# Two shared SBUF tags padded to 4608 bytes, so that the operands of the wide matmuls begin at one byte of a 512-byte line

## The chip, the cores and the metric

The kernel runs on one core of one Trainium2 chip. The metric is the device time of one execution in microseconds (us); lower is better. A core has a matrix engine (TensorE, PE in the profile, with its weight loads shown apart as PEld), VectorE (DVE), ScalarE (ACT), GpSimd (POOL) and SyncE (SP, which issues most of the DMAs here). SBUF, the on-chip memory that engines read their operands from, has 128 partitions; every tile is a run of bytes at the same start address in each of them.

## The reference, cut to what matters

Three stages follow each other on 8 x 3072 = 24576 rows of 256 values:

```
scores = (z @ z.T) / S;  attn = max(scores, 0)**2;  x = u * (attn @ v)         # S = 3072, z is 64 wide
xn = x / rms(x) * rms_g                                                        # 256 -> 1536 -> 256
x = (silu(xn @ w_gate) * (xn @ w_val)) @ w_out
keep = (x @ w_skip) > 0;  e = argmax(x @ gate);  p = softmax(x @ gate)[e]      # 8 experts, 256 -> 1024 -> 256
out = x;  out[keep] = x[keep] + p * (max(x[keep] @ w1[e], 0) @ w2[e])
```

## The kernel before, in words

The 24576 rows are worked in 48 chunks of 512 rows (CH). Every float32 operand of a large product is split into a rounded high part and the rest as a low part (`split`), and one product is three matmuls on TensorE (`mm3`, lines 231 to 233): high weights on high data, high weights on low data, low weights on high data. In each, the stationary operand (the weights) is a 128x128 tile, 512 bytes in each partition, and the moving operand is 512 columns wide, 2048 bytes in each partition. The score product (lines 566 and 567, `s<-z,z`) is two matmuls of the same shape. TensorE loads the weights of the next matmul while the one before it streams its moving operand.

The order is software-pipelined by hand: `Stream.unit` runs a front part (first product and its evictions) and, two units later, the back part (second product). The chunks go attention 0, attention 1, first MoE 0, attention 2, first MoE 1 and so on to first MoE 47. The profile's names for their matmuls:

- attention: 12 units for a chunk, each 4 matmuls `s<-z,z` and 12 matmuls `acc<-a,v` (moving `a`, weights `v`)
- first MoE: 12 units for a chunk, each 12 matmuls `gv<-xn,wg_s` and `gv<-xn,wv_s` (moving `xn`) and 6 matmuls `yacc<-h,wo_s` (moving `h`)
- second MoE (from about 4660 us on): groups, one per expert, with tiles of 512 and 256 rows, each with `h<-xh,w` (moving `xh`) and `y<-h,w` (moving `h`). Groups with an even number keep their weights in the tag `vhl`, odd ones in the tag `wodd` of the pool `p2`.

Tiles are given a tag in a pool. A tag gets as many buffers as `bufs` says, each as large as the largest tile that ever asks for that tag, and the tags of a pool lie one behind the other. So the size of one tag sets where every later tag begins. Of the pool `sp`, in the order of their places: `acct`, `u`, `vhl` (6 buffers; split `v`, the weights of even groups, `xh`, and `xn` of the last chunk), `zcat`, `stage`, `z1`, `z2` (the operands of the scores), `x`, `xn`, `hl` (5 buffers; `a` and `h`). Behind it lies the pool `wp` (`wg_s`, `wv_s`, `wo_s`), whose room the pool `p2` takes over for the second MoE.

Nearly all tags are whole multiples of 512 bytes. The tags `u` and `x` are 4096 bytes in almost all uses, but the first group of the second MoE loads its rows into them (line 888): 4 rows of XW = 265 values, 4240 bytes, and 4240 = 8 x 512 + 144 (the tags are laid out in steps of 32 bytes, so 4256 = 8 x 512 + 160 bytes lie between the start of `u` and of the next tag). The bytes below address 16384 of each partition are scratch in which GpSimd's own DMAs (`indirect_dma_start`, lines 703 and 945: the scatters into `xs` and `out`) keep their descriptors.

Of the kernel before, what the change touches and what calls it, by code (L numbers as in the profile page):

```python
# [10 lines left out]
F32 = mybir.dt.float32  # L11
# [9 lines left out]
P = 128  # L21
# [49 lines left out]
def tile_relu2_attention_moe_moe2(  # L71
# [15 lines left out]
    nc = tc.nc  # L87
# [15 lines left out]
    XW = D + E + 1  # L103
# [19 lines left out]
    sp = ctx.enter_context(tc.tile_pool(name="sp", bufs=1))  # L123
# [17 lines left out]
    for q, tag in ((0, "acct"), (1, "u")):  # L141
        g0, g1 = 4 * q, min(NCB, 4 * q + 4)
        if g0 < g1:
            t = sp.tile([P, g1 - g0, KT, DQ], F32, tag=tag, name=f"z0_{q}", bufs=1)
# [700 lines left out]
    class Group:  # L845
# [39 lines left out]
        def load_x(self, t):  # L885
            n = self.sizes[t] // P
            if self.i == 0 and t < 2:
                xt = sp.tile([P, n, XW], F32, tag=("u", "x")[t], name=f"xt_{self.i}_{t}", bufs=1)
            else:
                tag, bufs = ("xt", 3) if n == KT else ("xts", 5)  # L890
                xt = pools["p2"].tile([P, n, XW], F32, tag=tag, name=f"xt_{self.i}_{t}", bufs=bufs)
            if isinstance(self.e, int):
                r = self.e * RE + sum(self.sizes[:t])
            else:
                r = self.dyn(0, E * RE - TS)
            nc.sync.dma_start(xt, xs[ds(r, self.sizes[t]), :].rearrange("(p k) w -> p k w", k=n))
            self.xt[t] = xt
# [279 lines left out]
```

## Time and profile before

| | us |
|---|---|
| median of 3 runs | 5281.31 (5280.94 to 5281.61) |
| the profiled execution, its own time | 5281.5 |
| span of its instructions | 5279.6 |
| TensorE busy in the span | 5197.5 (98%), 23724 matmuls and transposes |
| weight loads busy | 4260.4 (81%) |
| VectorE, ScalarE, GpSimd busy | 3578.2 (68%), 2701.8 (51%), 426.8 (8%) |

How to read it: matmuls are pipelined, so the busy time of one matmul (about 390 ns) is longer than the time after which the next one starts (about 227 ns), and they overlap. The pace of a row of matmuls is the difference of their start times in the timeline. The granted clock is the share of TensorE's full clock that the chip granted; over the whole span it was 0.994.

### The profile page before, as it was taken

The page shows a single profiled execution, that of the slowest core. Times are in us where ns is not written, and L with a number is a line of the kernel's source. Part 1 is how long each engine was busy: PE and PEld are TensorE (multiplying, and loading weights), DVE is VectorE, ACT ScalarE, POOL GpSimd, SP SyncE. Part 2 cuts the span into 40 slices and gives each one's busy share as a digit, 9 for nine tenths or more (in the row PEclk, how much of TensorE's full clock was granted, in tenths as well). Part 3 has the DMA queues.
Part 4 walks back from the last instruction along what each step waited for, and adds up shares of the span by engine and source line. Part 5 has one row for each costly group of instructions (what it writes and reads, how often), then busy time and mean ns, then how long its engine had stood idle before and what let it go on. Part 6 is the DMA issues. An engine that isn't in the chain of part 4 may idle for free. (4 is left out here: it accounts for less than half of the span.)

```text
span 5279.6 us, 65890 instructions
## 1 busy us (share of the span) xinstructions
PE 5197.5 (98%) x23724; PEld 4260.4 (81%) x23724; DVE 3578.2 (68%) x8966; ACT 2701.8 (51%) x3559; POOL 426.8 (8%) x428
## 2 busy tenths in 40 slices
PE   7899999999999999999999999999999999999998
PEld 5688888888888888888888888878888888888888
DVE  8666767676677766776667667776677666544455
ACT  6445545465464554555546545455465554433344
POOL 5100000000000000000000000000000000021111
PEclk9999999999999999999999999999999999999999
DMA  5201101020011110111102001111011110122224
GB/s 163 54 19 41 43 20 36 19 62 23 19 36 35 41 27 19 42 43 23 32 19 66 19 19 36 38 40 25 19 42 43 24 31 18 41 85 84 79 95 155
DMA packets 547841, 234.43 MB, mean 44 GB/s; under 512 B 422357, under 2 KB 528000, under 8 KB 547384
## 3 DMA queue, kind: packets, MB, share of 16 engines
q1 hardware_dynamic: 533496, 205.00, 15.8%
q0 software_dynamic: 14016, 25.21, 1.4%
q8 instruction: 186, 3.05, 0.2%
q14 instruction: 143, 1.17, 0.1%
HBM read 144.79 MB, written 99.30 MB: 46 GB/s over the span
## 5 line engine op out<-in xcount | busy, mean ns | idle before, releaser
L738 ACT ACTIVATE gr<-gv 128x512 f32<-128x512 f32 x576 | 343.9, 597 | 1187.4 <-PE gv L233 1187.4
L232 PE MATMUL acc<-a,v 128*128 128x512 f32 x2304 | 916.6, 398 | 12.3 <-DVE a L228 8.5
L233 PE MATMUL acc<-a,v 128*128 128x512 f32 x2304 | 916.4, 398 | 0.0
L231 PE MATMUL acc<-a,v 128*128 128x512 f32 x2304 | 912.5, 396 | 1.6 <-ACT acct L427 1.6
L569 ACT ACTIVATE r<-s 128x1024 f32<-128x1024 f32 x576 | 590.9, 1026 | 339.2 <-PE s L567 319.8
L228 DVE TENSOR_TENSOR a<-r,a 128x512 fp32r<-128x512 f32 x1128 | 737.9, 695 | 23.4 <-ACT a L227 4.0
L654 DVE CUSTOM_DVE_ANT_0 jk<-ytok,wrb 128x256 bf16<-128x256 f32 x1656 | 697.9, 421 | 35.2
L739 DVE TENSOR_TENSOR gr<-gr,gv 128x512 f32<-128x512 f32 x576 | 394.8, 685 | 456.8 <-ACT gr L738 453.3
L228 DVE TENSOR_TENSOR h<-gr,h 128x512 fp32r<-128x512 f32 x576 | 399.1, 693 | 395.6 <-ACT h L227 395.6
L227 ACT CAST h<-gr 128x512 fp32r<-128x512 f32 x576 | 357.5, 621 | 573.8 <-DVE gr L739 573.8
L570 ACT ACTIVATE r<-r 128x1024 f32<-128x1024 f32 x576 | 611.5, 1062 | 18.2
L703 POOL DMA_INDIRECT xs<-ytok,pu x192 | 208.2, 1084 | 4128.3 <-DVE pu L701 3082.6
L232 PEld LDWEIGHTS acc<-a,v 128*128 128x128 f32 x2304 | 435.6, 189 | 120.1 <-DVE a L228 11.5
L231 PEld LDWEIGHTS acc<-a,v 128*128 128x128 f32 x2304 | 434.5, 189 | 107.0 <-ACT acct L427 2.1
L233 PEld LDWEIGHTS acc<-a,v 128*128 128x128 f32 x2304 | 434.6, 189 | 102.5
L225 DVE CAST a<-r 128x512 fp32r<-128x512 f32 x564 | 238.9, 424 | 379.1 <-ACT r L570 378.6
L231 PE MATMUL gv<-xn,wg_s 128*128 128x512 f32 x1152 | 457.0, 397 | 13.4 <-DVE gr L739 13.3
L567 PE MATMUL s<-z,z 128*128 128x512 f32 x1152 | 455.2, 395 | 0.1
L232 PE MATMUL gv<-xn,wg_s 128*128 128x512 f32 x1152 | 450.6, 391 | 1.1 <-DVE xn L228 1.1
L233 PE MATMUL yacc<-h,wo_s 128*128 128x512 f32 x1152 | 450.3, 391 | 0.6 <-POOL wo_s L376 0.6
L233 PE MATMUL gv<-xn,wg_s 128*128 128x512 f32 x1152 | 450.0, 391 | 0.0
L232 PE MATMUL yacc<-h,wo_s 128*128 128x512 f32 x1152 | 449.9, 391 | 0.0
(200 smaller groups left out, 9036.5 us busy)
## 6 DMA issues: line engine op xcount, KB each, us to landing
raw<-in_moe_w_dram SPq DMA_DIRECT2D x76, 512.0 KB
vn<-in_v_dram SPq DMA_DIRECT2D x48, 512.0 KB
out_dram<-ytok SPq DMA_DIRECT2D x48, 512.0 KB
ys<-yb SPq DMA_DIRECT2D x368, 64.0 KB
ytok<-ys SPq DMA_DIRECT2D x46, 512.0 KB
u<-in_u_dram SPq DMA_DIRECT2D x360, 64.0 KB
xs<-pad SPq DMA_DIRECT2D x8, 1325.0 KB
xt<-xs SPq DMA_DIRECT2D x16, 530.0 KB
```

The lines of the kernel that those rows point to most:

```text
L225: nc.vector.tensor_copy(hi, src)
L227: nc.scalar.copy(hi, src)
L228: (nc.vector if lo_eng == "v" else nc.gpsimd).tensor_sub(lo, src, hi.bitcast(F32))
L231: nc.tensor.matmul(ps, w_hi, x_hi, start=start, stop=False)
L232: nc.tensor.matmul(ps, w_hi, x_lo, start=False, stop=False)
L233: nc.tensor.matmul(ps, w_lo, x_hi, start=False, stop=stop)
L567: nc.tensor.matmul(ps[:, t], zj, zi2, start=False, stop=True)
L569: nc.scalar.activation(out=r, in_=ps, func=AF.Relu)
L570: nc.scalar.activation(out=r, in_=r, func=AF.Square)
L654: nc.vector.tensor_tensor_reduce(out=junk, in0=ytok[:, k, :D], in1=wrb[:, e, :], op0=ALU.mult, op1=ALU.add, scale=1.0, scalar=0.0, accum_o ...
L738: nc.scalar.activation(out=r[:, 0], in_=ps[:, 0], func=AF.Silu)
L739: nc.vector.tensor_mul(r[:, 1], r[:, 0], ps[:, 1])
```

## The change

The tile of line 888 is asked for as a run of 1152 values (9 x 128) in each partition, 4608 = 9 x 512 bytes, of which the first 1060 values are used as before. So the tags `u` and `x` grow from 4240 to 4608 bytes. The room comes from the scratch of GpSimd's DMAs, which goes from 16384 to 4096 bytes in each partition; everything behind it moves down by 12288 bytes (24 x 512). No instruction is added, removed or moved on any engine; what changes is where tiles lie. In the built programs the tiles begin, in bytes into their partition and, in brackets, into a line of 512 bytes:

| tag (tiles) | before | after |
|---|---|---|
| `r` (evicted scores, `gr`) | 33056 (288) | 20768 (288) |
| `acct` | 42592 (96) | 30304 (96) |
| `u` | 46688 (96) | 34400 (96) |
| `vhl` (`v`, even `w`, `xh`, last `xn`) | 50944 (256) | 39008 (96) |
| `stage` | 102144 (256) | 90208 (96) |
| `z1`, `z2` | 106240, 118528 (256) | 94304, 106592 (96) |
| `x` | 122624 (256) | 110688 (96) |
| `xn` | 126880 (416) | 115296 (96) |
| `hl` (`a`, `h`) | 135072 (416) | 123488 (96) |
| `wg_s`, odd `w` | 155552, 171936 (416) | 143968, 160352 (96) |
| `wv_s` | 180128 (416) | 168544 (96) |
| `wo_s` | 204704 (416) | 193120 (96) |

Buffers of one tag, the slices of 128 weights and the high and low parts lie whole multiples of 512 bytes apart, so the number in brackets holds for all of them. By it, the 128x512 matmuls of before are: `acc<-a,v` moving 416, weights 256; `gv` and `yacc` 416 and 416; `s` 256 and 256; in the second MoE, even groups `h` 256 and 256, `y` moving 416, weights 256; odd groups `h` moving 256, weights 416, `y` 416 and 416; the `gv` of the last chunk moving 256, weights 416. After the change all are 96 and 96.

```diff
@@ -885,7 +885,9 @@
         def load_x(self, t):
             n = self.sizes[t] // P
             if self.i == 0 and t < 2:
-                xt = sp.tile([P, n, XW], F32, tag=("u", "x")[t], name=f"xt_{self.i}_{t}", bufs=1)
+
+                room = sp.tile([P, -(-n * XW // P) * P], F32, tag=("u", "x")[t], name=f"xt_{self.i}_{t}", bufs=1)
+                xt = room[:, : n * XW].rearrange("p (n w) -> p n w", w=XW)
             else:
                 tag, bufs = ("xt", 3) if n == KT else ("xts", 5)
                 xt = pools["p2"].tile([P, n, XW], F32, tag=tag, name=f"xt_{self.i}_{t}", bufs=bufs)
@@ -1158,7 +1160,7 @@
-    nc = _bacc.Bacc("TRN2", target_bir_lowering=False, num_devices=1)
+    nc = _bacc.Bacc("TRN2", target_bir_lowering=False, num_devices=1, dynamic_dma_scratch_size=4096)
```

## Rows read from the trace of the kernel before

**Rows 1.** The page: span; TensorE's busy tenths and granted clock in 40 slices

```profile
span 5279.6 us, 65890 instructions
...
PE   7899999999999999999999999999999999999998
...
PEclk9999999999999999999999999999999999999999
```

**Rows 2.** Waits of TensorE: who, for whom, total us, times, longest

```profile
PE gv L231 <- DVE gr L739: 13.3, 1, 13.3
```

**Rows 3.** TensorE by shape: line, names, shape, count | busy us, mean ns

```profile
L232 PE MATMUL acc<-a,v 128*128 128x512 f32 x2304 | 916.6, 398 | 12.3 <-DVE a L228 8.5 <-POOL a L228 3.8
...
L231 PE MATMUL acc<-a,v 128*128 128x512 f32 x2304 | 912.5, 396 | 1.6 <-ACT acct L427 1.6
L231 PE MATMUL gv<-xn,wg_s 128*128 128x512 f32 x1152 | 457.0, 397 | 13.4 <-DVE gr L739 13.3
L567 PE MATMUL s<-z,z 128*128 128x512 f32 x1152 | 455.2, 395 | 0.1
...
L233 PE MATMUL yacc<-h,wo_s 128*128 128x512 f32 x1152 | 450.3, 391 | 0.6 <-POOL wo_s L376 0.6
...
L231 PE MATMUL yacc<-h,wo_s 128*128 128x512 f32 x1152 | 449.4, 390 | 0.3 <-ACT wo_s L375 0.3
...
L232 PE MATMUL gv<-xn,wv_s 128*128 128x512 f32 x1152 | 448.7, 390 | 0.0
L566 PE MATMUL s<-z,z 128*128 128x512 f32 x960 | 386.8, 403 | 5.5 <-ACT r L569 3.1 <-DVE gr L739 0.3
L231 PE MATMUL y<-h,w 128*128 128x512 f32 x256 | 102.3, 400 | 0.0
...
L232 PE MATMUL h<-xh,w 128*128 128x512 f32 x256 | 100.6, 393 | 0.0
...
L232 PE MATMUL h<-xh,w 128*128 128x256 f32 x288 | 81.3, 282 | 0.0
```

**Rows 4.** Timeline of TensorE, attention of chunk 20: start us, us, line, names

```profile
1959.74 0.39 PE L232 MATMUL acc<-a,v 128*128 128x512 f32 x1
...
1962.31 0.39 PE L566 MATMUL s<-z,z 128*128 128x512 f32 x1
...
1963.23 0.40 PE L231 MATMUL acc<-a,v 128*128 128x512 f32 x1
```

**Rows 5.** Timeline of TensorE, first MoE of chunk 46

```profile
4565.82 0.39 PE L233 MATMUL gv<-xn,wg_s 128*128 128x512 f32 x1
...
4569.22 0.39 PE L233 MATMUL yacc<-h,wo_s 128*128 128x512 f32 x1
```

**Rows 6.** Timeline of TensorE, first MoE of chunk 47

```profile
4625.81 0.39 PE L233 MATMUL gv<-xn,wg_s 128*128 128x512 f32 x1
...
4630.24 0.40 PE L231 MATMUL gv<-xn,wv_s 128*128 128x512 f32 x1
```

**Rows 7.** Stretches: length, busy of PE, PEld, DVE, ACT, POOL, clock, DMA, GB/s

```profile
1960.00:1965.00 5.00, 5.00 (x23) 4.05 (x22) 4.03 (x15) 3.95 (x5) 0.00 (x0) 1.00 0.00 0
...
4560.00:4590.00 30.00, 29.95 (x138) 24.59 (x137) 19.46 (x62) 9.80 (x16) 0.00 (x0) 1.00 0.00 1
4624.00:4654.00 30.00, 30.00 (x136) 24.17 (x135) 13.64 (x24) 11.20 (x17) 9.18 (x6) 1.00 0.08 26
```

**Rows 8.** TensorE by shape in 4760 to 4817 us, group 2

```profile
L233 PE MATMUL y<-h,w 128*128 128x512 f32 x32 | 12.7, 396 | 0.0
...
L233 PE MATMUL h<-xh,w 128*128 128x512 f32 x31 | 12.2, 392 | 0.0
```

**Rows 9.** TensorE by shape in 4820 to 4877 us, group 3

```profile
L233 PE MATMUL y<-h,w 128*128 128x512 f32 x32 | 12.5, 391 | 0.0
L233 PE MATMUL h<-xh,w 128*128 128x512 f32 x31 | 12.3, 397 | 0.0
```

**Rows 10.** GpSimd by line: the scatter into the output, and its idle time

```profile
L945 POOL DMA_INDIRECT out_dram<-ot,xt x100 | 101.0, 1010 | 479.6 <-DVE ot L940 270.1 <-DMA out_dram<-ot,xt 91.0 <-DVE h L981 42.3
```

## The prediction

> **What bounds the kernel now.** I read the page first. TensorE is busy in nine tenths or more of every slice but the first two and the last, and its granted clock is full in all 40 [rows 1]: the kernel is as long as its row of matmuls. The waits come next. The longest single wait of TensorE in the whole run is 13.3 us, once [rows 2]; so what remains is the pace at which one matmul follows another, and every nanosecond of pace counts, some 20,000 times.
>
> The view by shape shows that this pace is not one number. All the matmuls of 128x512 do the same amount of work, and still their mean durations range from 390 ns (`gv` on line 232) to 398 ns (`acc`) [rows 3]. Durations overlap, so I check against the timeline that a longer duration is a slower pace. In the attention of chunk 20 the 11 steps from 1959.74 to 1962.31 us are 2.57 us, 233.6 ns each [rows 4]; in the first MoE of chunk 46 the 15 steps from 4565.82 to 4569.22 us are 3.40 us, 226.7 ns each [rows 5]. 6.9 ns more in pace, against 7 to 8 in duration: the excess of a duration over 390 ns can be read as lost time.
>
> **Is the address the reason?** By the table of places, `gv` and `yacc` before have moving operand and weights at the same byte of a 512-byte line (416), `acc` has 416 against 256. That alone proves nothing, since attention differs in much else. Two places in the trace come close to an experiment.
>
> The first MoE of chunk 47 runs the same lines on the same weights as that of chunk 46, but its `xn` lies in `vhl`, at 256 against weights at 416. Its 19 steps from 4625.81 to 4630.24 us take 4.43 us, 233.2 ns each [rows 6], the pace of `acc`. VectorE is less busy there than in chunk 46 (13.64 us of 30 against 19.46), ScalarE about the same (11.20 against 9.80), the clock is full in both [rows 7]. Six of the 19 are `yacc`, at 416 and 416; had these the fast pace, the other 13 would take 236 ns each, more than any `acc` average, so an equal pair between unequal ones seems not to recover at once. GpSimd (9.18 us) and DMAs (share 0.08) are active there and not in chunk 46; but the attention units at 1960 to 1965 us have neither (0.00 and 0.00) and are slow [rows 7].
>
> In the second MoE the roles change from group to group. In group 2 (even) `h` has 256 and 256 and takes 392 ns, `y` has 416 against 256 and takes 396 [rows 8]. In group 3 (odd) `h` has 256 against 416 and takes 397, `y` has 416 and 416 and takes 391 [rows 9]. The swap follows the addresses and not the stage, and an equal pair is fast at 256 as it is at 416. After the change every pair is 96 and 96.
>
> **The change part by part.** No instruction is added, removed or moved, so no wait is added either. The terms are excesses over 390 ns.
>
> - `acc`: three rows, 912.5 to 916.6 us, together 2745.5 us for 6912 matmuls; 6912 x 0.390 = 2695.7; excess 49.8 us [rows 3]. All of it lies on the path, except in the first two slices, where TensorE is only 7 and 8 tenths busy and waits for other things [rows 1]; two of the 48 attention chunks run there, 2 us. Term: 48 us.
> - `gv`: six rows from 457.0 to 448.7 us, together 2705.1 us, excess 9.4 us; of this the first row (397 ns) alone has 7.7, and its matmuls come first in a unit and also bear the waits [rows 2, 3]. What is due to addresses is the last chunk (144 x 6.5 ns = 0.9 us) and the first matmuls after an `acc` that is still out of step. Between 2 and 9.4 us I take 5.
> - `yacc`: three rows, 449.4 to 450.3 us, 1349.6 in all, excess 1.8 us; I take 2.
> - `s`: equal at 256 before, yet 395 ns on line 567: they stand in fours between slow `acc`, as `yacc` did in chunk 47. Line 567: 455.2 - 1152 x 0.390 = 5.9 us. Line 566 is at 403 ns, 12.4 us over for 960 of its 1152, but it also waits for ScalarE to free the buffer [rows 3]. The timeline has 4 steps of `s` in 0.92 us, 230 ns, so (230 - 226.7) x 2304 = 7.6 us [rows 4]. Between 7.6 and 21 I take 8, the timeline's.
> - wide `h` and `y` of the second MoE: six rows from 102.3 to 100.6 us, 607.7 in all for 1536, excess 8.7 us [rows 3]; the rows of line 231 bear waits too. I take 7.
> - 128x256 matmuls: 1728, at 282 ns in the row shown [rows 3]. No row shows a fast and a slow one side by side. Bounds: nothing, and 7 ns on the half with unequal bytes, 864 x 7 = 6 us. I take nothing.
> - other engines: `r`, `acct` and `u`, from and to which most of the evictions go, keep their byte in the line; `a`, `h`, `v` and `xn` get another one. No row shows VectorE or ScalarE at two bytes for the same operation; I take nothing, and if they lost some time it would be covered: in the busiest attention units VectorE has 4.03 us of 5 and ScalarE 3.95 [rows 7], which at the faster pace become 4.15 and 4.07 of 5. The second product of a unit comes two units behind its first.
> - GpSimd's smaller scratch: scatters could wait for room. In the second MoE GpSimd already waits for the landing of its scatter before it issues the next (91.0 us of idle time), so hardly more than one is under way, and it is idle for 479.6 us between 100 scatters, 4.8 us for each [rows 10]. A wait below that costs nothing but at the very end, behind the last matmul: 0 to some 5 us. I take nothing.
>
> Sum: 48 + 5 + 2 + 8 + 7 = 70 us. The profiled execution took 5281.5 us around its span of 5279.6; 5281.5 - 70 = 5211.5, and as the median of the runs shown is 5281.31, I forecast 5211 us. What is late next is again TensorE, at an even pace of 227 ns.
>
> **The rivals.**
>
> No change. The pace of a stage could be set by what goes on beside TensorE (evictions, DMAs), and the addresses only happen to go with it. Then all terms are nothing: 5281 us. For it: attention does have the most traffic on VectorE and ScalarE. Against it: the pair of chunks 46 and 47, and the swap between groups 2 and 3. The Trainium skill speaks for this rival: TensorE: Matmul & The Clock Gate (Part 2, step by step) says that the weight load and the moving operand have separate read ports, so that loading the next weights takes no bandwidth from the running matmul, and SBUF — State Buffer (Who interferes with whom) says that TensorE never waits on anyone. By these pages no byte address could matter. The trace disagrees: 233.2 against 226.7 ns [rows 5, 6].
>
> Only part of it. Unequal bytes cost what `acc` shows, but `s`, `gv` and the second MoE are slow for other reasons (an evicted buffer, the groups' DMAs): then the gain is that of `acc` alone, 48 us, or less if `acc` settles between the two paces, say at 230 ns: 25 us. 5233 to 5257 us. For it: `s` is slow at 256 and 256.
>
> Slower: byte 96 itself is a bad one. No 512-wide matmul of before reads its operands from byte 96, and what I take for the difference of two bytes could be a property of certain start bytes. If 96 were of the slow kind, `gv`, `yacc` and the half of `h` and `y` now equal would go to the pace of `acc`: (233.3 - 226.7) x (6912 + 3456 + 768) = 73 us more, 5354 us. It decides as soon as an equal pair at 96 is slow. Against it: equal pairs are fast at both bytes where they occur, 256 and 416 [rows 8, 9].
>
> **How the numbers follow.** Forecast (an even pace everywhere) 0.83, part of it 0.08, no change 0.05, byte 96 bad (or the scratch felt beyond all the gain) 0.04. A difference under 0.2% (10.6 us) can't be told from none; so faster 0.91, same 0.05, slower 0.04. The range: with all upper ends (50 + 9.4 + 1.8 + 21 + 8.7 + 6) the gain would be 97 us, 5184; that all come together is unlikely, so 5192. Upward it takes in `acc` alone (5233) and a few us of the scratch: 5238.
>
> **What would show it.** Right: all rows of wide `acc`, `s`, `gv`, `yacc`, `h` and `y` at 389 to 392 ns but for the first of a unit; steps of 227 ns in an attention unit; `yacc` and `gv` as before; chunks 46 and 47 alike; the scatters' idle time on GpSimd shorter by about what TensorE gains and their durations as before. Wrong: `acc` still at 397 ns (traffic, not addresses), or `gv` and `yacc` at 397 (byte 96), or TensorE's pace even but its waits longer by tens of us (the gain given back to VectorE or ScalarE), or waits of GpSimd before each scatter.

## The result, and the profile after

The changed kernel takes 5212.19 us (median of 4 runs, 5209.95 to 5214.61) against 5281.46 us of the kernel before (4 runs, 5280.94 to 5281.82): a ratio of 0.987, 95% interval 0.9858 to 0.9882. The forecast was 5211 us. The execution that was profiled took 5214.61 us around its span, 66.9 us less than the profiled execution of before.

The page first (span; TensorE's busy tenths; its granted clock). It answers to [rows 1]: as many instructions, the same shape of the span, the same clock. Only the length is another.

```profile
span 5212.8 us, 65890 instructions
...
PE   7899999999999999999999999999999999999998
...
PEclk9999999999999999999999999999999999999999
```

TensorE by shape (line, names, shape, count | busy us, mean ns of one | idle before). It answers to [rows 3].

```profile
L232 PE MATMUL acc<-a,v 128*128 128x512 f32 x2304 | 900.3, 391 | 12.7 <-DVE a L228 8.8 <-POOL a L228 3.8
L231 PE MATMUL acc<-a,v 128*128 128x512 f32 x2304 | 899.1, 390 | 1.7 <-ACT acct L427 1.7
L233 PE MATMUL acc<-a,v 128*128 128x512 f32 x2304 | 898.9, 390 | 0.0
L231 PE MATMUL gv<-xn,wg_s 128*128 128x512 f32 x1152 | 455.2, 395 | 13.7 <-DVE gr L739 13.6
L567 PE MATMUL s<-z,z 128*128 128x512 f32 x1152 | 452.4, 393 | 0.1
L233 PE MATMUL yacc<-h,wo_s 128*128 128x512 f32 x1152 | 449.4, 390 | 0.6 <-POOL wo_s L376 0.6
...
L232 PE MATMUL gv<-xn,wv_s 128*128 128x512 f32 x1152 | 448.6, 389 | 0.0
...
L566 PE MATMUL s<-z,z 128*128 128x512 f32 x960 | 385.1, 401 | 5.7 <-ACT r L569 3.1 <-DVE gr L739 0.3
...
L231 PE MATMUL y<-h,w 128*128 128x512 f32 x256 | 101.4, 396 | 0.0
...
L232 PE MATMUL h<-xh,w 128*128 128x512 f32 x256 | 99.8, 390 | 0.0
...
L232 PE MATMUL h<-xh,w 128*128 128x256 f32 x288 | 81.4, 283 | 0.0
```

`acc` fell from between 396 and 398 ns to 390 and 391, the duration that `gv` and `yacc` had before and still have. What stands above that now are the first `gv` and the first `y` of a unit and `s` on line 566, which also wait, and `s` on line 567 at 393 ns. By the starts in the trace, an `s` whose four stands between `acc` takes 226.7 ns from its start to the next one; a four beside `yacc` or beside the small transposes takes 227 to 231.

The timeline of an attention unit (start us, duration us, line, names) answers to [rows 4].

```profile
1929.63 0.39 PE L231 MATMUL acc<-a,v 128*128 128x512 f32 x1
...
1932.35 0.39 PE L566 MATMUL s<-z,z 128*128 128x512 f32 x1
...
1933.26 0.39 PE L231 MATMUL acc<-a,v 128*128 128x512 f32 x1
```

From 1929.63 to 1933.26 us are 16 steps, 12 `acc` and 4 `s`: 3.63 us, 226.9 ns each, where before an `acc` step took 233.6 ns. The first MoE of chunk 47, the slow twin in [rows 6], has become like its neighbour in [rows 5]; from its timeline:

```profile
4565.63 0.39 PE L233 MATMUL gv<-xn,wv_s 128*128 128x512 f32 x1
...
4567.67 0.39 PE L233 MATMUL yacc<-h,wo_s 128*128 128x512 f32 x1
```

9 steps in 2.04 us, 226.7 ns each (before, 233.2).

Little was given back. The longest wait of TensorE, in the view of waits, is 13.6 us [13.3 in rows 2]; in a busy attention unit, in the view of stretches, VectorE and ScalarE have 4.50 and 4.05 us of 5 (the columns are those of [rows 7]), and TensorE is busy for all 5:

```profile
PE gv L231 <- DVE gr L739: 13.6, 1, 13.6
```

```profile
1930.00:1935.00 5.00, 5.00 (x24) 4.14 (x23) 4.50 (x16) 4.05 (x5) 0.00 (x0) 1.00 0.00 0
```

One thing else moved. Behind the last matmul GpSimd ends the program with DRAIN instructions. The view of that line shows count, shortest / median / longest in ns, first and last start; first the kernel before, then after:

```profile
L1173 POOLq DRAIN  x3: 40/103/6601, 5272.2 to 5279.4; - x3
```

```profile
L1175 POOLq DRAIN  x3: 40/103/1619, 5210.3 to 5212.5; - x3
```

The longest fell from 6.60 to 1.62 us, on the path that sets the end. I had not looked at it. The scatters before it (GpSimd by line) wait 85.1 us for their landings where it was 91.0, and take 993 ns where it was 1010 [rows 10]: the small scratch held none of them up.

```profile
L947 POOL DMA_INDIRECT out_dram<-ot,xt x100 | 99.3, 993 | 477.1 <-DVE ot L942 245.6 <-DMA out_dram<-ot,xt 85.1 <-DVE w L228 48.7
```

### The profile page after: what moved, and what is told of

It is laid out like the page before. It is cut to its first block, busy times and chain, and to the rows that moved or that the text cites. A ratio compares the mean times of both kernels' runs of the same rounds, so it can differ in the third digit from the quotient of the medians.

```text
span 5212.8 us, 65890 instructions
## 1 busy us (share of the span) xinstructions
PE 5132.3 (98%) x23724; PEld 4258.5 (82%) x23724; DVE 3576.1 (69%) x8966; ACT 2705.3 (52%) x3559; POOL 427.3 (8%) x428
## 5 line engine op out<-in xcount | busy, mean ns | idle before, releaser
L232 PE MATMUL acc<-a,v 128*128 128x512 f32 x2304 | 900.3, 391 | 12.7 <-DVE a L228 8.8
L231 PE MATMUL acc<-a,v 128*128 128x512 f32 x2304 | 899.1, 390 | 1.7 <-ACT acct L427 1.7
L233 PE MATMUL acc<-a,v 128*128 128x512 f32 x2304 | 898.9, 390 | 0.0
L231 PE MATMUL gv<-xn,wg_s 128*128 128x512 f32 x1152 | 455.2, 395 | 13.7 <-DVE gr L739 13.6
L232 PE MATMUL gv<-xn,wg_s 128*128 128x512 f32 x1152 | 449.4, 390 | 1.1 <-DVE xn L228 1.1
L233 PE MATMUL yacc<-h,wo_s 128*128 128x512 f32 x1152 | 449.4, 390 | 0.6 <-POOL wo_s L376 0.6
L231 PE MATMUL yacc<-h,wo_s 128*128 128x512 f32 x1152 | 449.3, 390 | 0.4 <-ACT wo_s L375 0.4
L232 PE MATMUL yacc<-h,wo_s 128*128 128x512 f32 x1152 | 449.0, 390 | 0.0
```

Of the source, the lines that this page charges most:

```text
L231: nc.tensor.matmul(ps, w_hi, x_hi, start=start, stop=False)
L232: nc.tensor.matmul(ps, w_hi, x_lo, start=False, stop=False)
L233: nc.tensor.matmul(ps, w_lo, x_hi, start=False, stop=stop)
```

## The experiments

The theory: the pace is lost where moving operand and weights lie at different bytes of a line. Rivals: the traffic beside TensorE, byte 96 as such, the scratch, and a shorter line. Where it says "one run" there is a single time; the times of one kernel spread over some 5 us.

### The two halves of the change, and another common byte

Scratch alone: the kernel before with

```diff
+    nc = _bacc.Bacc("TRN2", target_bir_lowering=False, num_devices=1, dynamic_dma_scratch_size=4096)
```

> The smaller scratch alone; the two tags stay at 4240 bytes, so all tiles keep the bytes of before (416, 256, 96). Theory 'equal bytes' (a matmul is fast when moving operand and weights begin at the same byte of a 512-byte line): acc stays at 397 ns, 5281 us, at most 5 us less because GpSimd's drain at the very end (6.6 us before, 1.6 us after) may go with the scratch. Rival 'scratch' (room or reads of the smaller scratch give the gain): 5212 us, acc at 390 ns.

Measured: 5276.26 us (10 runs, 5273.61 to 5278.14) against 5281.79 (19 runs); ratio 0.9989 (0.9979 to 0.9999). By shape, `acc` keeps its slow pace, and in the view of the last line the drain is as short as in the changed kernel:

```profile
L233 PE MATMUL acc<-a,v 128*128 128x512 f32 x2304 | 917.4, 398 | 0.0
```

```profile
L1173 POOLq DRAIN  x3: 40/103/1619, 5272.8 to 5275.0; - x3
```

The scratch by itself brings 5.5 us, of which the drain is 5.0 (6.60 - 1.62).

Padding alone: the changed kernel with a scratch that just leaves it room.

```diff
-    nc = _bacc.Bacc("TRN2", target_bir_lowering=False, num_devices=1, dynamic_dma_scratch_size=4096)
+    nc = _bacc.Bacc("TRN2", target_bir_lowering=False, num_devices=1, dynamic_dma_scratch_size=15360)
```

> The two tags padded, the scratch at 15360 bytes, nearly the default (the whole default does not leave room for the padding); all tiles at byte 96 as in the changed kernel. 'Equal bytes': acc at 390 ns, 5212 us, up to 5 us more if the drain at the end goes with the scratch. 'Scratch': 5281 us.

Measured: 5221.25 us (4 runs, 5217.12 to 5222.15), ratio 0.9883 (0.9867 to 0.9900). The pace is wholly there; what is missing is at the end:

```profile
L233 PE MATMUL acc<-a,v 128*128 128x512 f32 x2304 | 899.9, 391 | 0.0
```

```profile
L1175 POOLq DRAIN  x3: 40/103/7744, 5211.2 to 5219.5; - x3
```

So padding alone brings 60.5 us and the scratch alone 5.5, in sum 66; the whole brought 69.3 (5281.46 - 5212.19). The 3 us between are within the spread, and 1.1 of them lie in the drain, which is longer with 15360 bytes than with 16384 (7.74 against 6.60 us).

All operands at byte 0 instead of 96: the changed kernel with 416 unused bytes ahead of everything.

```diff
-    snap = cpool.tile([P, 2], F32, name="snap")
+    snap = cpool.tile([P, 106], F32, name="snap")[:, :2]
```

> The changed kernel with 416 unused bytes ahead of all tiles of the products, so that every operand begins at byte 0 of a line instead of 96. 'Equal bytes': 5212 us, acc and all wide matmuls at 390 ns as at 96. Rival 'a certain byte' (start bytes are fast or slow by themselves, 96 being a fast one): some rows off 390 ns; if 0 were of the kind of 256 in the scores of before (395 ns), 5215 to 5285 us.

Measured: 5213.95 us (4 runs, 5211.44 to 5214.64), ratio 0.9871 (0.9854 to 0.9887). By shape:

```profile
L233 PE MATMUL acc<-a,v 128*128 128x512 f32 x2304 | 900.0, 391 | 0.0
```

As fast as at 96. Between these two bytes it doesn't matter which one it is, only that it is the same for both.

### Only the weights of acc moved, by five distances

If the addresses are the cause, it must be possible to take the gain of `acc` back without touching attention's work. In the changed kernel the tag `vhl` (`v`, and with it even `w` and `xh`) moves up by d bytes, and a later tag takes up the rest of the 512, so that all other operands lie as after the change (d = 352 here; 256, 128, 64 and 32 with their own numbers):

```diff
-                room = sp.tile([P, -(-n * XW // P) * P], F32, tag=("u", "x")[t], name=f"xt_{self.i}_{t}", bufs=1)
+                room = sp.tile([P, -(-n * XW // P) * P + (88, 0)[t]], F32, tag=("u", "x")[t], name=f"xt_{self.i}_{t}", bufs=1)
-        cat = sp.tile([P, KT, 2, DQ], F32R, tag="zcat", name=f"zc_{b}_{g}", bufs=1)
+        cat = sp.tile([P, KT * 2 * DQ + 40], F32R, tag="zcat", name=f"zc_{b}_{g}", bufs=1)
+        cat = cat[:, : KT * 2 * DQ].rearrange("p (k a d) -> p k a d", a=2, d=DQ)
```

> The changed kernel with the tag vhl (v, even weights, xh, the last xn) moved to byte 448 and everything else left at 96: for acc the difference of the bytes, moving less weights, is 160 in the line again, as in before, while the scores (96 and 96) and the first MoE stay equal. 'Equal bytes': acc back at 397 ns (+48 us), the scores slow again by what they get from their neighbours (393 to 395 ns, +4 to +8 us), half of the second MoE and the last gv slow: 5265 to 5280 us. Rival 'each matmul for itself' (an equal pair is fast whatever stands beside it): the scores stay at 392 ns or below, 5262 us or less. 'A certain byte': acc anywhere between 390 and 397 ns.

Measured: 5273.61 us (10 runs, 5270.75 to 5275.57), ratio 0.9985 (0.9976 to 0.9995). By shape:

```profile
L231 PE MATMUL acc<-a,v 128*128 128x512 f32 x2304 | 919.4, 399 | 1.6 <-ACT acct L428 1.6
...
L568 PE MATMUL s<-z,z 128*128 128x512 f32 x1152 | 455.6, 396 | 0.1
```

All of the gain but 8 us (5281.79 - 5273.61), 5 of them the drain's, is gone: `acc` lies at 96 and 448 and has the slow pace again. `s`, at 96 and 96, is slow with it (396 against 393 ns), so "each matmul for itself", which asked for 5262 us or less, is out.

The line of 512 bytes was taken from the table of places, not shown. At 256 bytes apart:

> The tag vhl alone moved by 256 bytes, to byte 352 of a line, everything else at 96. 'Equal bytes of a 512-byte line': acc at 396 to 398 ns, steps of 233 to 235 ns, about 5273 us. Rival 'shorter line' (the line that matters is 256 bytes long or less): acc at 390 ns, 227 ns, 5212 us.

Measured: 5213.46 us, one run. Here the theory failed in the length of its line, and the rival with the shorter line was right. By shape and from the timeline:

```profile
L233 PE MATMUL acc<-a,v 128*128 128x512 f32 x2304 | 899.6, 390 | 0.0
```

```profile
1930.13 0.39 PE L231 MATMUL acc<-a,v 128*128 128x512 f32 x1
...
1933.75 0.39 PE L231 MATMUL acc<-a,v 128*128 128x512 f32 x1
```

16 steps in 3.62 us, 226.3 ns: two operands 256 bytes apart count as equal.

> The tag vhl alone moved by 128 bytes, to byte 224. 'Equal bytes of a 512-byte line': acc slow, steps of 231 to 235 ns, 5255 to 5275 us. 'Shorter line' of 128 bytes: 227 ns, 5212 us.

> The tag vhl alone moved by 64 bytes, to byte 160. 'Equal bytes': acc slow, steps of 231 to 235 ns if any difference costs the same. 'Shorter line' of 64 bytes: 227 ns, 5212 us. Rival 'distance' (the loss grows with the distance of the bytes): between 227 and 231 ns, 5215 to 5250 us.

> The tag vhl alone moved by 32 bytes, to byte 128. 'Equal bytes' with any difference costing the same: acc at 231 to 235 ns a step, 5255 to 5275 us. 'Distance': nearer to 227 ns than at 64 bytes, below 5235 us.

Measured, one run each: 5269.73, 5265.37 and 5263.54 us; the kernel before, run once beside them, took 5286.0 us. By shape at 128, 64 and 32 bytes:

```profile
L233 PE MATMUL acc<-a,v 128*128 128x512 f32 x2304 | 913.5, 396 | 0.0
```

```profile
L233 PE MATMUL acc<-a,v 128*128 128x512 f32 x2304 | 911.8, 396 | 0.0
```

```profile
L233 PE MATMUL acc<-a,v 128*128 128x512 f32 x2304 | 912.7, 396 | 0.0
```

Worked out from all starts in the traces, the mean `acc` step is 234.0 ns at 352, 226.8 at 256, and 233.1, 233.1 and 232.9 at 128, 64 and 32. The distance hardly matters: 32 bytes cost 51 us against the changed kernel (5263.5 - 5212.4), 64 cost 53, 128 cost 57 and 352, which is 96 modulo 256, cost 61; in the traces `acc` alone takes 41 us more than in the changed kernel at 32 bytes and 48 at 352. Distances under 32 bytes were not run.

### Which two bytes must agree

In `acc` the weights of one matmul and of the next lie at the same byte, so the runs so far don't tell whether a matmul is slowed by its own weights or by those that are loaded beside it for the next. This kernel moves `z1`, `z2` alone, by 160 bytes: `s` has 256 and 256, `acc` 96 and 96, and every matmul agrees with its own weights.

```diff
-                room = sp.tile([P, -(-n * XW // P) * P], F32, tag=("u", "x")[t], name=f"xt_{self.i}_{t}", bufs=1)
+                room = sp.tile([P, -(-n * XW // P) * P + (0, 88)[t]], F32, tag=("u", "x")[t], name=f"xt_{self.i}_{t}", bufs=1)
-        cat = sp.tile([P, KT, 2, DQ], F32R, tag="zcat", name=f"zc_{b}_{g}", bufs=1)
+        cat = sp.tile([P, KT * 2 * DQ + 40], F32R, tag="zcat", name=f"zc_{b}_{g}", bufs=1)
+        cat = cat[:, : KT * 2 * DQ].rearrange("p (k a d) -> p k a d", a=2, d=DQ)
```

> The changed kernel with the operands of the scores (z1 and z2) both moved by 160 bytes, to byte 256; everything else stays at 96. Every matmul has an equal pair, but in attention four at 256 stand between twelve at 96. Theory 'order' (the matmuls keep their pace while stream and weight load beside it begin at equal bytes, and after a break need some matmuls to get it back): the matmul that loads the first weights of the other kind is late, and 2 or 3 behind it too; twice in each of 576 units some 10 to 15 ns, so the scores at 229 to 232 ns a step, acc at 228 to 229, 5222 to 5232 us. Rival 'each matmul for itself': all at 227 ns, 5212 us.

Measured: 5235.73 us, one run, a few us above what the theory gave and 24 above what "each for itself" gave. The timeline across one `s` group:

```profile
1936.04 0.39 PE L232 MATMUL acc<-a,v 128*128 128x512 f32 x1
...
1937.40 0.39 PE L232 MATMUL acc<-a,v 128*128 128x512 f32 x1
1937.63 0.40 PE L233 MATMUL acc<-a,v 128*128 128x512 f32 x1
1937.87 0.39 PE L567 MATMUL s<-z,z 128*128 128x512 f32 x1
...
1938.80 0.40 PE L231 MATMUL acc<-a,v 128*128 128x512 f32 x1
...
1939.49 0.39 PE L231 MATMUL acc<-a,v 128*128 128x512 f32 x1
1939.72 0.39 PE L232 MATMUL acc<-a,v 128*128 128x512 f32 x1
...
1941.30 0.40 PE L233 MATMUL acc<-a,v 128*128 128x512 f32 x1
1941.54 0.39 PE L567 MATMUL s<-z,z 128*128 128x512 f32 x1
```

The 6 steps of `acc` from 1936.04 to 1937.40 take 1.36 us, 226.7 ns each. The last `acc`, whose next weights are `z`, takes 0.24 us; the 4 `s` take 0.93 (232.5 each), the first 3 `acc` 0.69 (230), the rest, from 1939.72 to 1941.30, 226 each. As means over all groups: last `acc` 236.6 ns; the four `s` 229.2, 233.3, 235.8 and, with the next weights `v`, 235.0; then `acc` 232.5, 230.8, 227.4. By shape:

```profile
L233 PE MATMUL acc<-a,v 128*128 128x512 f32 x2304 | 902.5, 392 | 0.0
...
L568 PE MATMUL s<-z,z 128*128 128x512 f32 x1152 | 459.0, 398 | 0.1
```

`s` is slower than anywhere else, though its own pair is equal. The first late step is the `acc` beside which the weights of `s` are loaded. But at this border the moving operand goes to another byte too, which could as well be the cause. Two other runs tell the two apart, since in them every moving operand of attention and of the first MoE but that of the last chunk stays at 96. In the run with `v` moved by 32 bytes, `s` has 96 and 96, and only the last of its four has weights at another byte loaded beside it (`v`, 128):

```profile
1946.89 0.39 PE L567 MATMUL s<-z,z 128*128 128x512 f32 x1
...
1947.57 0.40 PE L568 MATMUL s<-z,z 128*128 128x512 f32 x1
1947.81 0.39 PE L231 MATMUL acc<-a,v 128*128 128x512 f32 x1
```

Three steps in 0.68 us, 226.7 ns each, then 0.24 us; as means over 406 groups 230.6, 226.9, 227.0 and 234.8 ns. The other is the run below. So it is enough that the weights loaded meanwhile begin at another byte than the moving operand, and after such a disagreement it takes some matmuls to get back in step. That fits `s` in the kernel before, slow at 256 and 256 behind the unequal pairs of `acc`. Which of the steps at a border is late isn't the same for all distances (at 352 bytes the last `s` takes 228.4 ns and the third `acc` behind it 237.4); that order isn't explained.

The other way round: the weights of the first MoE moved by 160 bytes.

```diff
-    wg_s = wp.tile([P, 2, DH, F1], F32R, name="wg_s")
+    wg_s = wp.tile([P, 2 * DH * F1 + 40], F32R, name="wg_s")
+    wg_s = wg_s[:, 40:].rearrange("p (a h f) -> p a h f", a=2, h=DH)
```

> The changed kernel with the weights of the first MoE (wg_s, wv_s, wo_s) moved by 160 bytes, to byte 256, against xn and h at 96; attention and the second MoE stay at 96 and 96. Theory 'equal bytes': the loss that acc had before is put into gv and yacc, which never had it: both at 396 to 398 ns, steps of 233 to 234 ns, acc at 390 ns; 10368 x 6.5 ns = 67 us more than 5212, 5275 to 5285 us. Rival 'only attention feels it' (its traffic on VectorE and ScalarE is needed for the loss): gv and yacc stay near 390 ns, 5212 to 5230 us.

Measured: 5285.06 us, one run. By shape:

```profile
L233 PE MATMUL acc<-a,v 128*128 128x512 f32 x2304 | 899.5, 390 | 0.0
...
L232 PE MATMUL gv<-xn,wv_s 128*128 128x512 f32 x1152 | 456.5, 396 | 0.0
...
L232 PE MATMUL yacc<-h,wo_s 128*128 128x512 f32 x1152 | 456.3, 396 | 0.0
```

The loss can be put into a stage that never had it: `gv` and `yacc` step at 233.3 and 233.4 ns. `acc` stays fast but at its border with `gv`, where the weights of `gv`, at 256, are loaded beside the last `acc`, with no moving operand at another byte:

```profile
1976.53 0.39 PE L233 MATMUL acc<-a,v 128*128 128x512 f32 x1
...
1977.21 0.40 PE L233 MATMUL acc<-a,v 128*128 128x512 f32 x1
1977.45 0.39 PE L231 MATMUL gv<-xn,wg_s 128*128 128x512 f32 x1
```

Three steps in 0.68 us, then 0.24; over all 141 such borders the last `acc` takes 236.6 ns, the three before it 226.8. This stage has less traffic on VectorE than attention (13.64 to 19.46 us of 30 against 4.03 of 5 [rows 7]), and no instruction of it changed: traffic isn't the cause. Of the 73 us more (5285.06 - 5212.36), 68 lie in the steps of `gv` and `yacc`, as the expectation gave it (67), and 5 in `acc` beside them. That the prediction has 73 too, for byte 96 as a bad one, is chance: its sum counts the wide `h` and `y` of the second MoE, which this run leaves equal.

### Again, and once more of the same

To close the series the changed kernel, with no edit, ran once more:

> The changed kernel once more, to be compared with the next one on the same chip: 5212 us, wide matmuls at 390 ns, drain of GpSimd at the end 1.6 us.

Measured: 5212.36 us (4 runs, 5210.94 to 5214.28), ratio 0.9869 (0.9853 to 0.9886) against 5282.61 (7 runs): the first result stands.

One operand left at another byte is the identity of the 128x128 transposes. With it equal too modulo 256, and half the scratch:

```diff
-    identr = cpool.tile([P, P], F32R, name="ident")
+    identr = cpool.tile([P, P + 64], F32R, name="ident")[:, 56 : 56 + P]
-    nc = _bacc.Bacc("TRN2", target_bir_lowering=False, num_devices=1, dynamic_dma_scratch_size=4096)
+    nc = _bacc.Bacc("TRN2", target_bir_lowering=False, num_devices=1, dynamic_dma_scratch_size=2048)
```

> The changed kernel with the scratch at 2048 bytes and the identity of the 128x128 transposes moved from byte 128 to byte 96 of a 256-byte line, as all wide operands. If the drain of GpSimd at the end goes with the scratch (6.6 us at 16384, 1.6 us at 4096), it is 0.8 to 1.2 us. If the transposes follow the rule of the wide matmuls, zps steps fall below 84 ns and the scores behind them keep their pace: 1 to 3 us. Together 1 to 4 us below the changed kernel; rival: neither moves, 5212 us. If scatters ran out of room in the smaller scratch, GpSimd would wait longer before each.

Measured: 5214.66 us (4 runs, 5212.78 to 5215.61), ratio 0.9871 (0.9855 to 0.9888): no gain over the change, where 1 to 4 us were expected. Equal bytes bring the transposes nothing that can be seen: `zps` starts come 82.0 ns apart, against 82.5 in the run before (medians). The drain is shorter again, by 0.57 us, which is less than the spread:

```profile
L1175 POOLq DRAIN  x3: 40/103/1047, 5211.9 to 5213.5; - x3
```

## Why the prediction was right, by its steps

The mechanism held, and so did the sum of its terms; that the whole agrees as closely as it does is partly luck. All starts of wide matmuls in the two traces give each family's loss directly. "Pace" is the mean step between starts, without steps over 260 ns (which hold waits), times the count; "all steps" is the difference of the sums with the waits in them:

| term | forecast, us | pace, us | all steps, us | step before, after, ns |
|---|---|---|---|---|
| `acc` | 48 | 48.8 | 46.6 | 233.9, 226.8 |
| `gv` | 5 | 4.8 | 5.9 | 227.5, 226.8 |
| `yacc` | 2 | 1.9 | 1.4 | 227.7, 227.1 |
| `s` | 8 | 6.6 | 5.1 | 230.4, 227.5 |
| wide `h`, `y` | 7 | 6.0 | 5.5 | 231.8, 227.9 |
| sum | 70 | 68.1 | 64.5 | |
| scratch, at the end | 0 (priced 0 to 5 as a cost) | | 5 gained | |

- *Reading durations over 390 ns as lost time* was sound: by rows `acc` got 2745.5 - 2698.3 = 47.2 us shorter, by pace 48.8, with its waits 46.6.
- *`gv`*: the loss did sit behind attention, as the prediction argued: the first six `gv` and `yacc` behind it came at 228 to 232.5 ns before and at 226.7 to 228.1 after.
- *`s`*: the 8 us were taken against 226.7 ns; its steps come down to 227.5, and line 567 to 393 ns where 389 to 392 was named as the sign. Of the upper end (21 us), line 566's 12.4, nearly all stayed: 401 ns where it was 403. It waits, as the prediction said it might.
- *128x256 matmuls*: priced at nothing, and the row shown has 282 ns before and 283 after. By the table of places half of them had unequal bytes before (starts 119.4 ns apart on average, waits left out, and 119.8 after), so in so short a matmul no loss shows.
- *Other engines*: nothing, as priced: VectorE is busy for 3576.1 us after and 3578.2 before, ScalarE for 2705.3 and 2701.8 (the page). The prediction took 4.03 and 3.95 us of 5 for the busiest attention unit; from 1930 to 1935 us before they have 4.83 and 4.65 (view of stretches), so there was less room than it says.
- *Waits*: the prediction has none added. From the first matmul to the last the run is 61.9 us shorter, so waits and the small matmuls took back some 6 us of the 68.1. The changed kernel run once more has 64.9, so about half of that may be spread.
- *The clock*: the prediction read it as full in all 40 slices, but a 9 stands for nine tenths or more. From 4598 to 4618 us it was 0.83 before, and 0.83 after from 4540 to 4560 us (view of stretches): the same dip in both, and no part of the gain.
- *Scratch*: the step that failed. I asked whether scatters would wait for room and took 0 from 0 to 5 us of cost. They don't wait, and the end of the program gets 5 us shorter instead (6.60 to 1.62 us). So the agreement of 70 forecast and 69.3 measured is partly luck: two things that weren't in the sum, some 6 us given back and 5 us of drain gained, nearly cancel. What is left of the pace, 61.9, and the drain, 5, make the 66.9 of the profiled pair.
- *Rivals*: "no change" (traffic) falls by the runs in which only a base address moves, in either stage; "only `acc`" by `s` and the second MoE; "byte 96" by the run at byte 0. By what the prediction cites of the Trainium skill (TensorE: Matmul & The Clock Gate, Part 2, step by step; SBUF — State Buffer, Who interferes with whom) the runs with moved weights would be as fast as the changed kernel; they are 61 and 73 us slower.
- *The line*: the prediction read "equal" by lines of 512 bytes. By the runs it is 256; before, the pairs differed by 160 bytes either way, so the forecast didn't depend on it.

Open: why a weight load and the stream beside it want the same byte; nothing in the profile names a conflict, and the weight loads themselves take 188 ns (median) for `acc` before and after. The kernel with `vhl` 352 bytes up is 2.7 us faster than that with the small scratch alone; by the traces `gv` and `yacc` take 4.6 us less in it (2383.4 against 2388.0), as behind attention they are back at 227 ns after two late steps where the other needs six. Why it gets back in step sooner is not explained.

## What to carry to other kernels

Where TensorE is the bound and matmuls of one shape show two durations (here float32 ones of 128x512; those of 128x256 showed no loss), list the start addresses of moving operand and weights modulo 256 and make them equal over the whole chain, also across the borders between kinds of matmul; a border costs some matmuls on both sides. Test such a reading by moving one tile by a few bytes, in both directions, before the story is believed. And with every change of a resource, look at the last microseconds of the program as well.

## What was not expected of the hardware

- Two operands 256 bytes apart run at full pace (226.3 ns), and 32 bytes cost nearly as much as 352 (232.9 against 234.0 ns).
- Equal pairs are slow beside equal pairs at another byte: up to 235.8 ns for `s` with 256 and 256 between `acc` at 96 and 96.
- The last DRAIN of GpSimd goes with the scratch of its DMAs, though not in proportion: 1.05 us at 2048 bytes, 1.62 at 4096, 7.74 at 15360, 6.60 at 16384.
